# Backward of an attention and MLP block: dS of four units transposed in two transfers instead of one

## The chip, the core and the metric

The kernel runs on one core of one Trainium2 chip. A core has a matrix engine (TensorE, PE in the profile), a vector engine (VectorE, DVE), an engine for activation functions (ScalarE, ACT), a general one (GpSimd, POOL) and one that mostly issues transfers (SyncE, SP). Sixteen DMA engines move data between the chip's memory and the core's own memories, and within those; a transfer can transpose blocks of two-byte numbers on its way. The metric is the device time of one execution in microseconds. Before the change it is 2510.57 us, the median of three runs (2510.35 to 2513.57).

## The reference

One block of a transformer with adaptive layer norm is computed forward and backward, in bf16: 2048 tokens, width 512, 32 heads of 16, an MLP of width 1792. The outputs are the block's result and nine gradients. Cut to the part that matters, the forward of the attention is

```python
qkv = (x @ wqkv).reshape(B, S, 3, H, Dh)       # S = 2048, H = 32, Dh = 16
scores = jnp.einsum('bhqd,bhkd->bhqk', q, k) * scale
p = jax.nn.softmax(scores, axis=-1)
o = jnp.einsum('bhqk,bhkd->bhqd', p, v)
```

and the gradients come from `jax.vjp` of the whole block. For one head the backward needs, with P the softmax and dO the gradient of o:

- dP = dO V^T, and dS = P * (dP - the row sum of dO * O);
- dV = P^T dO and dK = dS^T Q, which contract over the queries;
- dQ = dS K, which contracts over the keys.

The matrix engine contracts over the partition dimension. dS is made with queries on the partitions, which serves dK; for dQ each 128x128 block of it has to be transposed, so that keys are on the partitions.

## The kernel before

The program runs through a forward phase, the MLP's backward, the attention's backward (`phase5` and `attn_bwd`), and a last phase with the weight gradients (`phase6`). Only the attention's backward is touched.

**Loops.** `attn_bwd` walks over 8 groups of four heads (`g`), two pairs of heads in each (`jp`), 4 chunks of 512 keys (`c`), and 16 tiles of 128 queries (`ib`). One step of the innermost loop is a *unit*: 128 queries, 512 keys, two heads (`a` = 0, 1). Four units in a row are a *group* (G = 4); there are 256 groups. Two groups in a row are a *pair*, 128 in all.

**A unit.** For each of its two heads PE makes the scores (L1601) and ACT their exponential `pu` (L1604). One unit later PE makes dP (L1522, in `dP`), and DVE multiplies it with `pu` into `ds` (L1526). In every second group (`off`) the product of unit 1, head 1, is made by ACT and POOL instead: ACT copies dP out of PSUM (L1534), POOL multiplies (L1535, in `dP_pool`). Matmuls for dK and dV follow (L1459, in `kv`).

**A group's dS.** The tile `ds` has 128 partitions (queries) and 4 units x 2 heads x 512 keys, that is 32 blocks of 128x128, eight to a unit. There are three such buffers. `dS` is called one unit behind the scores; when it is called for the last unit of a group, which is in the first unit of the next group, it issues one transposing transfer on SP (L1543) from `ds` to a tile `dsT`. In groups that are not `off` the transfer leaves out blocks 0 to 3 (unit 0, head 0): `turn_ds`, called in the third unit of a group, has PE transpose these four (L1559) and ACT copy them to `dsT` (L1560). So the transfer has 28 blocks in even groups and 32 in odd ones (`off`, where `turn_ds` only chooses the buffer). A block is 32 KB.

**dQ.** When both groups of a pair have been sent off, eight entries join the list `pendq`. `dq` takes one entry and issues four matmuls (L1484), each of which reads one half of one of the pair's two `dsT` tiles. Two entries are taken in the first and the third unit of each group, as long as more than eight are in the list. A pair's matmuls therefore begin two groups after its second transfer was issued and are spread over two groups. The last of them gives its two `dsT` tiles back to the list `dT_free`, which holds five tiles in all (four of its own, and one in the tile `keep`); `turn_ds` takes the first free one.

**The order.** PE, SP and POOL run their instructions in the order in which the program is written (a manual schedule). In this stage SP's queue holds nothing but the transfers of dS. POOL's queue holds its products and the loads for the next heads (L1590), each behind a one-element copy `tick` (L1589) that ties it to a `ds`. After the loops POOL issues eight loads of 128 KB (L1623), PE works off what is left of dK, dV and dQ between the first matmuls of the weight gradients (L1652), and DVE brings the last dQ out of PSUM (L1492).

**Waits.** The tile framework puts them in: a transfer waits for the engines that wrote its blocks and for the readers of the tile it overwrites, and a reader of `dsT` waits for the transfer that wrote the part it reads.

Of the kernel before, what the change touches and what calls it, by code (L numbers as in the profile page):

```python
# [19 lines left out]
P = 128  # L20
# [15 lines left out]
class Background:  # L36
# [13 lines left out]
    def next(self):  # L50
        while self.gens:
            r = next(self.gens[0], None)
            if r is not None:
                if isinstance(r, tuple):
                    self.mark = r[0]
                    self.seen.add(r[0])
                return r
            self.gens.pop(0)
        return None
# [46 lines left out]
class K:  # L106
# [1324 lines left out]
    def attn_bwd(self):  # L1431
# [7 lines left out]
        tc, nc = self.tc, self.nc  # L1439
        S, D, H, NQ, ST, SC = self.S, self.D, self.H, self.NQ, self.ST, self.SC  # L1440
        G = 4
# [95 lines left out]
        def dS(u):  # L1537

            (T, g, jp, c, ib, kvT, pu, dsg, i, grp) = u
            pend.append((T, g, jp, c, ib, kvT, pu, dsg[:, i]))  # L1540
            if i == G - 1:
                dsT, n = grp
                nc.sync.dma_start_transpose(dsT.rearrange("p (b k) -> p b k", k=P)[:, n:, :],  # L1543
                                            dsg[:].rearrange("p i a k -> p (i a k)")[:, n * P:])
                two.append(dsT)
                if len(two) == 2:
                    pendq.extend((T, g, jp, c, ib - 2 * G + 1, a, sub, two[:]) for a in range(2) for sub in range(4))
                    two.clear()

        def turn_ds(dsg, grp, skip, late):  # L1550

            dsT = next(t for t in dT_free if not late or t is not own)
            dT_free[:] = [t for t in dT_free if t is not dsT]
            grp.extend((dsT, 0 if skip else 4))
            if skip:
                return
            tp = stp.tile([P, 4, P], BF16, name="st")
            for b in range(4):
                nc.tensor.transpose(tp[:, b, :], dsg[:, 0, 0, b * P:(b + 1) * P], self.ident[:])  # L1559
            nc.scalar.copy(dsT[:, 0:4 * P], tp[:].rearrange("p b k -> p (b k)"))  # L1560
# [4 lines left out]
        for g in range(NQ):  # L1565
            for jp in range(2):
# [16 lines left out]
                for c in range(SC):  # L1583
                    c0 = 512 * c
                    for ib0 in range(0, ST, G):
# [5 lines left out]
                        dsg, grp = self.dsp.tile([P, G, 2, 512], BF16, name="ds"), []  # L1591
                        for i in range(G):
                            ib = ib0 + i
                            q = slice(ib * P, (ib + 1) * P)
                            if turnq and i == 3 and m >= (7 if turnq[0][2] is None else 2):
                                turn(*turnq.pop(0))
                            pu = self.pup.tile([P, 2, 512], BF16, name="pu")
                            for a in range(2):
                                stt = stp.tile([P, 512], F32, name="st")
                                rs = slice(64 * jp, 64 * jp + 64)  # L1600
                                nc.tensor.matmul(stt[:], lhsT=T["QT"][rs, q], rhs=masked["KT"][a][rs, c0:c0 + 512],  # L1601
                                                 start=True, stop=True)
                                held = dP(last, a) if last else None
                                nc.scalar.activation(pu[:, a, :], stt[:], ACT.Exp, scale=self.scale)  # L1604
                                if held is not None:
                                    dP_pool(last, held)
                                if a == 0 and i % 2 == 1 and off(c, ib) and len(pend) >= 4:
                                    kv_two(1)
                            if last:
                                dS(last)  # L1610
                            last = (T, g, jp, c, ib, kvT, pu, dsg, i, grp)
                            if i % 2 == 1 and len(pend) >= 4:
                                kv_two(1 if off(c, ib) else 2)
                            elif i % 2 == 0 and len(pendq) > 2 * G:
                                for _ in range(4 if end else 2):
                                    dq(pendq.pop(0))
                            if i == 2:
                                turn_ds(dsg, grp, off(c, ib), end and m > 2)
            T = Tn
        with tc.manual_schedule(engines=ALL):  # L1620
            for t in (2, 0):
                for p in self.wq_pieces(t):
                    nc.gpsimd.dma_start(*p)  # L1623
            for a in range(2):
                dP(last, a)
            dS(last)
            while len(pend) > 2:
                kv_two()
            kv_two(1)
            for _ in range(2 * G):  # L1630
                dq(pendq.pop(0))
            kv_two(1)
            k0, v0, k1 = [dpp.tile([P, 512], F32, name="dp") for _ in range(3)]
            self.dw_mm(k0, 1, 0, 0, ST // 2)
            turn(*turnq.pop(0))
            self.dw_mm(v0, 2, 0, 0, ST // 2)
            self.dw_mm(k0, 1, 0, ST // 2, ST)
            self.col_sum(1)
            self.dw_mm(v0, 2, 0, ST // 2, ST)
            self.col_sum(2)  # L1640
            self.cs_bc(1)
            while pendq:
                dq(pendq.pop(0))
            self.cs_bc(2)
            turn(*turnq.pop(0))
            self.dw_mm(k1, 1, 1, 0, ST)
# [312 lines left out]
```

## Time and profile before

| | |
|---|---|
| median of three runs | 2510.57 us (2510.35 to 2513.57) |
| the profiled execution | 2511.14 us, its span 2509.0 us |
| busy share of the span | PE 97%, ACT 91%, DVE 68%, POOL 29% |
| the attention's backward | first transfer of dS at 1174.8 us, last at 2385.4 us |
| transfers of dS | 256: 208 to the tiles `dsT`, 48 to the one in `keep` |
| from issue to landing, those to `dsT` | 5.0 / 6.7 / 8.8 us (least, median, greatest) |
| SP's queue held by one, the same | 3.4 / 4.1 / 6.3 us |
| data moved by DMA | 445.78 MB, of which 336.29 MB on SP's queue |

All times inside an execution are counted from the start of the span. The profile lists instructions by source line, and the same line can stand for thousands of them. "PE accq L1484 <- DMA dsT<-ds" reads: PE stood still before a matmul of line 1484 that writes `accq`, and what ended the wait was the landing of a transfer from `ds` to `dsT`. A duration of a transfer on SP's queue is the time in which the queue is held by the issue; the landing is later. The DMA share is the mean over the sixteen engines of the time that their packets took, and can exceed 1 because packets overlap; GB/s is what they moved.

### The profile page before, as it was taken

Reading aid. Unit: us, or ns where it says so; the run is one execution under the profiler, and the core shown is the slowest. Engines: PE = TensorE matmul, PEld = TensorE weight load, DVE = VectorE, ACT = ScalarE, POOL = GpSimd, SP = SyncE. Lnnn points to the kernel's source line nnn. Section 1 sums busy time; section 2 is a strip of 40 time slices with the busy share of each in tenths; the row PEclk is TensorE's granted clock in tenths of the full one; section 3 lists DMA queues with packets and bytes.
Section 4 is the critical chain, followed back from the end, with each engine's and each line's share of the span. In section 5 each row is a group of like instructions: output and inputs, shape, how many; then the busy total and the mean of one; then the engine's idle time right before and its main releaser. Section 6 shows DMA issues by size and latency. Waiting matters only on the chain.

```text
span 2509.0 us, 68721 instructions
## 1 busy us (share of the span) xinstructions
PE 2438.6 (97%) x26695; PEld 1080.0 (43%) x26695; DVE 1709.6 (68%) x3519; ACT 2295.0 (91%) x3789; POOL 716.4 (29%) x1289
## 2 busy tenths in 40 slices
PE   8999999999999999999999999999999999999998
PEld 4555555555555554573333333333333333333343
DVE  6222322422332344677999999999999999999957
ACT  7999999999999997534999999999999999999935
POOL 2344531220131022245222222222222222222223
PEclk9999999999999999999999999999999999999999
DMA  4688661441243044598999999999999999999997
GB/s 166 133 180 208 170 121 50 129 100 39 99 115 90 23 131 138 122 199 214 236 215 227 224 221 228 223 222 221 229 222 222 230 223 222 225 226 232 233 191 208
DMA packets 1260526, 445.78 MB, mean 178 GB/s; under 512 B 1204052, under 2 KB 1228246, under 8 KB 1260198
## 3 DMA queue, kind: packets, MB, share of 16 engines
q1 hardware_dynamic: 1219654, 336.29, 70.7%
q0 software_dynamic: 38464, 104.04, 13.6%
q8 instruction: 209, 3.42, 0.6%
q10 hardware_dynamic: 2080, 1.05, 0.1%
q14 instruction: 119, 0.97, 0.1%
HBM read 75.83 MB, written 64.49 MB: 56 GB/s over the span
## 4 chain that ended last, share of the span: by engine, by line
PE 58%; ACT 27%; DMA 7%; issue 4%; DVE 3%; POOL 1%; SPq 0%; DVEq 0%; ACTq 0%; POOLq 0%
ACT pu L391 18%; PE st L1601 17%; PE acckv L1459 8%; PE st L388 8%; ACT pu L1604 7%; PE accq L1484 5%; DMA dsT<-ds 3%; PE accbank L322 3%; PE dps L1050 2%; PE pps L1237 2%; PE st L1559 1%; PE dp L1522 1%; PE dp L1652 1%; DVE ds L1526 1%; DMA keep<-ds 1%
## 5 line engine op out<-in xcount | busy, mean ns | idle before, releaser
L1526 DVE TENSOR_TENSOR ds<-dp,pu 128x512 bf16<-128x512 f32 x1920 | 1181.7, 684 | 25.1 <-PE dp L1522 19.1
L1604 ACT ACTIVATE pu<-st 128x512 bf16<-128x512 f32 x2048 | 1072.7, 661 | 30.1 <-PE st L1601 21.3
L391 ACT ACTIVATE pu<-st 128x1024 bf16<-128x1024 f32 x992 | 912.2, 1077 | 5.1 <-PE st L388 4.9
L388 PE MATMUL st<-QTm,KTq 128*128 128x512 bf16 x1984 | 588.4, 377 | 20.0 <-ACT pu L391 6.0
L322 PEld LDWEIGHTS <-pu 128*128 128x128 bf16 x8192 | 347.3, 96 | 236.3 <-issue 3.2
L1522 PE MATMUL dp<-kvm,q 64*128 64x512 bf16 x1024 | 364.1, 384 | 1.5 <-DVE ds L1526 0.7
L1522 PE MATMUL dp<-kvm,dOTg 64*128 64x512 bf16 x1024 | 361.8, 384 | 0.5 <-DVE ds L1526 0.4
L322 PE MATMUL accbank<-Vaug,pu 128*128 128x17 bf16 x8192 | 357.7, 171 | 1.2 <-ACT Vaug L522 0.9
L1601 PE MATMUL st<-kvm,q 64*128 64x512 bf16 x1024 | 351.6, 381 | 6.0 <-ACT pu L1604 0.2
L1601 PE MATMUL st<-kvm,QTg 64*128 64x512 bf16 x1024 | 350.6, 381 | 6.8
L388 PEld LDWEIGHTS <-KTq 128*128 128x128 bf16 x1984 | 188.2, 96 | 177.5 <-issue 125.6
L1535 POOL TENSOR_TENSOR ds<-junk,pu 128x512 bf16<-128x512 f32 x64 | 73.8, 1153 | 372.2 <-ACT junk L1534 302.4
L1459 PE MATMUL acckv<-ds,Qg 128*16 128x512 bf16 x1024 | 176.0, 382 | 0.2
L1459 PE MATMUL acckv<-pu,dOg 128*16 128x512 bf16 x1024 | 175.9, 382 | 0.0
L1459 PE MATMUL acckv<-ds,q 128*16 128x512 bf16 x1024 | 175.8, 382 | 0.0
L1459 PE MATMUL acckv<-pu,q 128*16 128x512 bf16 x1024 | 175.8, 382 | 0.0
L1535 POOL TENSOR_TENSOR ds<-csq,pu 128x512 bf16<-128x512 f32 x64 | 73.8, 1154 | 349.6 <-ACT csq L1534 271.5
L302 POOL DMA_DIRECT2D QTm<-QTq_d x124 | 63.8, 516 | 341.5 <-PE st L388 319.9
L1601 PEld LDWEIGHTS <-q 64*128 64x128 bf16 x1024 | 66.9, 94 | 159.6 <-issue 144.0
L1601 PEld LDWEIGHTS <-QTg 64*128 64x128 bf16 x1024 | 67.0, 94 | 158.2 <-issue 141.3
L329 DVE RECIPROCAL rl<-accbank 128x4 f32<-128x4 f32 x128 | 23.0, 179 | 159.0 <-PE accbank L322 158.8
L1522 PEld LDWEIGHTS <-q 64*128 64x128 bf16 x1024 | 89.8, 93 | 56.7 <-issue 50.4
(390 smaller groups left out, 3197.0 us busy)
## 6 DMA issues: line engine op xcount, KB each, us to landing
KTq<-KTq_d POOLq DMA_DIRECT2D x24, 512.0 KB, 3.8
duT_d<-auT POOLq DMA_DIRECT2D x3, 1792.0 KB, 7.6
aT_d<-rT POOLq DMA_DIRECT2D x3, 1792.0 KB, 11.0
KTq_d<-KTq SPq DMA_DIRECT2D x32, 128.0 KB, 2.1
QTq_d<-ev_fm SPq DMA_DIRECT2D x32, 128.0 KB, 4.3
ktm_d<-ev_tm POOLq DMA_DIRECT2D x32, 128.0 KB, 2.5
VTq_d<-vT POOLq DMA_DIRECT2D x4, 1024.0 KB, 6.2
dx<-dx_d SPq DMA_DIRECT2D x16, 256.0 KB, 5.3
```

The source lines that it names most:

```text
L302: nc.gpsimd.dma_start(QTm[j][32 * j:32 * j + 32, :], self.QTq_d[g, 32 * j:32 * j + 32, 512 * qc:512 * (qc + 1)])
L322: nc.tensor.matmul(acc[:, a, sub, :], lhsT=pu[:, a, sub * P:(sub + 1) * P], rhs=Vaug[:, kb, h, :], start=(kb == 0 and a == 0 and sub == 0) ...
L388: nc.tensor.matmul(stt[:, a, :], lhsT=KT[:, kb * P:(kb + 1) * P], rhs=QTm[2 * jp + a][:], start=True, stop=True)
L391: nc.scalar.activation(pu[:], stt[:], ACT.Exp, scale=self.scale)
L1050: nc.tensor.matmul(pt[:], lhsT=a[st], rhs=g_tm[:, st, :], start=(st == 0), stop=(st == ST - 1))
L1459: nc.tensor.matmul(acckv[r:r + DH, :], lhsT=T[n][:, ib, col:col + DH], rhs=src[:, a, :], start=(ib == 0), stop=(ib == ST - 1))
L1484: nc.tensor.matmul(accq[r:r + 32, o:o + 256], lhsT=T["K"][:, 4 * c + sub, col:col + 32], rhs=v[:, r // 32 % 2 * 2:r // 32 % 2 * 2 + 2, 4 * ...
L1522: nc.tensor.matmul(dp[:], lhsT=T["dOT"][rd, ib * P:(ib + 1) * P], rhs=masked["VT"][a][rd, 512 * c:512 * (c + 1)], start=True, stop=True)
L1526: nc.vector.tensor_tensor(dsg[:, i, a], dp[:], pu[:, a, :], ALU.mult)
L1535: nc.gpsimd.tensor_tensor(dsg[:, i, 1], f[:], pu[:, 1, :], ALU.mult)
L1601: nc.tensor.matmul(stt[:], lhsT=T["QT"][rs, q], rhs=masked["KT"][a][rs, c0:c0 + 512], start=True, stop=True)
L1604: nc.scalar.activation(pu[:, a, :], stt[:], ACT.Exp, scale=self.scale)
```

## The change

The one transfer of a group becomes two. The first carries units 0 and 1 (12 blocks where the first four go over PE, else 16) and is issued in `turn_ds`, in the third unit of the group, ahead of PE's four transposes. The second carries units 2 and 3 (16 blocks) and is issued where the one transfer was. A helper `cross` issues both. The matmuls of dQ, the buffers and the order on the other engines stay as they are.

```diff
             if i == G - 1:
                 dsT, n = grp
-                nc.sync.dma_start_transpose(dsT.rearrange("p (b k) -> p b k", k=P)[:, n:, :],
-                                            dsg[:].rearrange("p i a k -> p (i a k)")[:, n * P:])
+                cross(dsg, dsT, 4 * G, 8 * G)
                 two.append(dsT)
...
+        def cross(dsg, dsT, a, b):
+            nc.sync.dma_start_transpose(dsT.rearrange("p (b k) -> p b k", k=P)[:, a:b, :],
+                                        dsg[:].rearrange("p i a k -> p (i a k)")[:, a * P:b * P])
+
         def turn_ds(dsg, grp, skip, late):
 
             dsT = next(t for t in dT_free if not late or t is not own)
             dT_free[:] = [t for t in dT_free if t is not dsT]
             grp.extend((dsT, 0 if skip else 4))
+            cross(dsg, dsT, grp[1], 4 * G)
             if skip:
                 return
```

## The prediction

> **What bounds the kernel now.** I read the profile in this order: busy time by stage, then the waits inside the stage that the change touches, then the transfer itself (how long it takes, what the DMA engines move meanwhile), then the tail of the stage. The stage is the attention backward, from about 1175 to 2390 us.
>
> Busy time by engine in a stretch of it (columns: stretch, length, busy us of each engine with instruction counts, granted clock, DMA share, GB/s):
>
> ```profile
> 1180.00:2384.00 1204.00, 1185.66 (x12962) 385.25 (x12958) 1179.06 (x1917) 1194.81 (x2438) 313.61 (x627) 1.00 1.18 225
> ```
>
> ScalarE (fourth) is busy for 1194.81 of 1204 us; TensorE, 1185.66, and VectorE, 1179.06, are close behind. No engine can lose work through this change, so what it can give is waits. The waits of ACT and PE on others in the same stretch, and the longest of SP's queue (total us, times, longest):
>
> ```profile
> ACT pu L1604 <- PE dp L1522: 5.3, 12, 0.9
> PE accq L1484 <- DMA dsT<-ds: 3.8, 8, 0.9
> PE accq L1484 <- DMA keep<-ds: 0.9, 2, 0.5
> SPq L1543 <- DVE ds L1526: 584.9, 226, 5.4
> ```
>
> ACT stands still for 5.3 us in the whole stage. PE has ten waits on a landing dS, together 4.7 us, and they stand behind ACT's: the matmuls of dQ (L1484) hold up the scores that ACT needs. SP has time: its queue waits 584.9 us for VectorE. Then the transfer: the transposes of dS, 28 or 32 blocks of 128x128, beside a small transpose of 4 blocks from the forward (columns of the first two kinds of line: duration min/median/max in ns, here the time that SP's queue is held; the last is issue to landing in us):
>
> ```profile
> L1543 SPq DMA_TRANSPOSE dsT<-ds x208: 3399/4099/6260, 1174.8 to 2385.4; - x104
> DMA to landing us min/median/max: 5.0/6.7/8.8
> L646 SPq DMA_TRANSPOSE ev_tm<-KTq x32: 1189/1202/2556, 61.2 to 244.2; - x32
> DMA to landing us min/median/max: 2.3/3.2/5.4
> ```
>
> The shortest landings give (5.0 - 2.3) / (28 - 4) = 0.11 us a block, and 2.3 - 4 x 0.11 = 1.85 us that does not depend on size. One such transfer, with a product of POOL that its group needs, in half-microsecond stretches:
>
> ```profile
> 1603.88 1.15 POOL L1535 TENSOR_TENSOR ds<-csq,pu 128x512 bf16<-128x512 f32 x1 [5.44 <-ACT csq L1534]
> ...
> 1605.97 4.81 SPq L1543 DMA_TRANSPOSE dsT<-ds  x1
> ```
>
> ```profile
> 1606.00:1606.50 0.50, 0.50 (x11) 0.20 (x4) 0.50 (x2) 0.50 (x2) 0.00 (x0) 1.00 0.34 81
> 1606.50:1607.00 0.50, 0.50 (x12) 0.12 (x8) 0.50 (x2) 0.50 (x2) 0.18 (x1) 1.00 0.30 107
> ...
> 1608.50:1609.00 0.50, 0.50 (x8) 0.20 (x4) 0.50 (x2) 0.50 (x2) 0.00 (x0) 1.00 0.03 3
> 1609.00:1609.50 0.50, 0.50 (x12) 0.12 (x8) 0.50 (x2) 0.50 (x2) 0.00 (x0) 1.00 0.09 10
> ...
> 1610.00:1610.50 0.50, 0.48 (x6) 0.18 (x3) 0.50 (x2) 0.50 (x2) 0.00 (x0) 1.00 1.28 291
> ...
> 1612.50:1613.00 0.50, 0.50 (x10) 0.16 (x6) 0.50 (x1) 0.50 (x3) 0.00 (x0) 1.00 1.33 247
> ```
>
> Read the last column. After the issue at 1605.97 the rate is low for a microsecond, there is a second hole at 1608.5 to 1609.5, and then 290 GB/s. The next transfer, issued at 1610.88 while this one was still moving, leaves hardly a hole where it takes over (247 at 1612.5). Holes belong to a start from rest. Last, the end of the stage, in the chain that ended last and in PE's timeline: the final dQ matmuls wait for the final transfer.
>
> ```profile
> 2385.37 14.00 DMA dsT<-ds
> ```
>
> ```profile
> 2399.41 1.05 PE L1484 MATMUL accq<-dsT,Kg 128*32 128x256 bf16 x30 [2.52 <-DMA dsT<-ds]
> ```
>
> **The change part by part.** A group of four units lasts 1210.6 us / 255 = 4.75 us (first to last issue of L1543), a pair of groups 9.5. The instructions of PE, ACT, DVE and POOL and their order do not change; SP gets 256 transposes more.
>
> *The earlier first half.* In even groups it has 12 blocks and is ready when DVE has made units 0 and 1, two units or 2.4 us ahead of the end. In odd groups it has 16 blocks and needs POOL's half of unit 1: in the rows above that ends at 1603.88 + 1.15 = 1605.03, only 0.94 us before the issue at 1605.97. The odd group is the one that counts: its dS is wanted two groups (9.5 us) after its last matmul, the even group's one group later still.
>
> *The landing of the pair's last blocks.* The 32 blocks of the odd group start 0.94 us earlier and follow each other at 0.11 us a block, so the end moves forward by 0.94 less what the second start costs. That is 0.1 us if it is queued behind the first (rate 247 instead of 290 for half a microsecond: 0.07), and 0.6 if it leaves half of the one-microsecond hole. Ends: a gain of 1.8 us (16 blocks x 0.11, the whole first half out of the way) and a loss (below, the second rival). I take 0.7, near the queued row, since the second half will be issued while the first still moves.
>
> *The waits in the stage.* With 0.7 us less, all waits of PE on dS up to 0.7 go and one of 0.9 leaves 0.2; of ACT's 5.3 us I take 4.4 as gained. Bounds: 0 and 5.3. What is late next is ACT itself.
>
> *The tail.* PE waits 2.52 us for a transfer that takes 14.00 us beside eight loads of 128 KB (POOL, L1623), with which it shares the engines whatever the order. I take 0.6, nearly the 0.7 above; bounds 0 and 2.5.
>
> *SP.* Two issues of at least 1.19 us (the 4-block row) in place of one of 3.4 to 4.1. If the hold goes with the blocks still to be moved, the sum stays near 4.1 of 4.75 us; nothing but these transposes is in SP's queue in this stage, so the second half waits behind the first and nobody else does. In odd groups the first half also waits for the dQ matmuls that have just freed its buffer; they precede POOL's product by over a microsecond.
>
> *Waits on other engines.* The first ds of a buffer on DVE, POOL's product and the dQ matmuls wait for two transfers instead of one. A satisfied wait is a semaphore instruction of some 20 ns that runs under the one before it (DVE is busy 98% with a wait at every instruction), so nothing. PE's transposes of unit 0 and ACT's copy to blocks 0 to 3 write other blocks than the first half; nothing.
>
> *Sum.* 4.4 + 0.6 = 5.0 us. The profiled execution took 2511.14 us (span 2509.0), 0.57 over the median of 2510.57. Against it 2506.1; against the median 2505.6. A measurement of this kernel can tell about 0.2%, 5.0 us, from no change, so this lies on the edge of it.
>
> *A rule against the change.* The Trainium skill, "DMA: Bandwidth & Descriptors" (Rules for kernel authors), says to coalesce many small transfers into one, and under "Anatomy of one DMA" gives about 2.0 us fixed for a transfer, for a software-generated one. That agrees with the 1.85 us from the rows. By the page alone 256 transfers more would be 512 us of fixed cost, if none of it overlapped; by the rows, where SP is free at 3.4 us and the blocks land at 5.0, most of it lies beside the transfer before.
>
> **The rivals.**
>
> *The DMA engines become the bound (slower).* A pair moves 60 blocks, 60 x 0.11 = 6.75 us; all traffic is 225 GB/s x 9.5 us = 2.14 MB, of which the blocks are 1.97, so loads take 0.17 MB or 0.6 us at 290 GB/s. That leaves 9.5 - 6.75 - 0.6 = 2.15 us, now filled with the holes of two transfers. With four transfers the point is 2.15 / 4 = 0.54 us a transfer: under it all is as above, over it each pair is late and PE, ACT and DVE wait for dS every time. At 0.6 us a start the price is 4 x 0.6 - 2.15 = 0.25 us a pair, over 128 pairs 32 us: 2542. At 1.07 (what two starts cost now) it would be 273 us. For it: the stage already moves 225 of 290 GB/s, and loads of POOL come in at the joints. Against it: the joint at 1612.5.
>
> *It is hidden anyway, or does not do what it says.* In odd groups the head start is only 0.94 us; if the joint eats it (0.6 for a hole, 0.3 for a load that slips between the halves), the landing does not move and neither do the waits. Time 2510 +- 3.
>
> *All waits go.* 5.3 + 2.5 = 7.8 us, 2502.8: the first half clears the way entirely. The 14.00 us at the tail, shared with loads, speaks against the second part.
>
> **How the numbers follow.** Waits go, mostly or all: 0.52, times 2502.5 to 2508, of which 0.32 is beyond 0.2%. Hidden: 0.18, nearly all within 0.2%. DMA bound: 0.30, from 2512 up, 0.28 of it beyond. Together faster 0.32, same 0.39, slower 0.29. The range begins at all waits gone, 2502.8, rounded down; upwards I leave out about half of the DMA case, that beyond 0.58 us a start (4 x 0.58 - 2.15 = 0.17, x 128 = 22 us): 2533. The likeliest case by itself is 2502.5 to 2508.
>
> **What would show it.** Right: twice the issues on the transpose's line, landings of the second half at 4 to 6 us, the ten waits of PE on dS down to one or two, ACT's 5.3 us under 1.5, the tail's 2.52 us under 2. Wrong: PE's wait on dS in tens of microseconds with landings of 8 us and more and a GB/s that stays near 225 (the DMA bound), or the same ten waits (hidden). The price of a joint between two halves is the step most likely to fail.

## The result, and the profile after

The changed kernel takes 2515.64 us (median of 20 runs, 2509.49 to 2521.17) where the kernel before took 2509.80 (20 runs beside them, 2502.70 to 2516.53). The ratio is 1.0021, 95% interval 1.0013 to 1.0030: some 5.3 us slower (5.8 by the medians). The prediction was 2505.6, 5.0 us faster; its range (2502.5 to 2533) holds the time, its direction is wrong.

The profiled execution after is the shortest of its twenty (2509.49 us, span 2507.7), 1.65 us under that of before. So the two are compared by stage, not by span, and the trace shows less of the loss than the median has. From the start to the first exponential of the backward (L1604, now L1608): 1168.31 before, 1165.62 after; nothing was changed there. From the first to the last of these exponentials: 1215.17 and 1218.40, that is 3.2 us longer. From there to the end: 125.54 and 123.71.

After, the stretch of the prediction's first view (columns as there):

```profile
1180.00:2384.00 1204.00, 1183.14 (x12938) 384.11 (x12935) 1174.72 (x1913) 1192.05 (x2431) 311.51 (x625) 1.00 1.20 225
```

ACT, the fourth, is busy for 2.8 us less of the same 1204. After, the waits of the same stretch (total us, times, longest):

```profile
ACT pu L1608 <- PE dp L1522: 7.8, 13, 1.8
PE accq L1484 <- DMA dsT<-ds: 5.6, 9, 1.4
SPq L1550 <- DVE ds L1526: 703.6, 372, 4.1
SPq L1550 <- POOL tick L1593: 171.1, 117, 3.6
```

PE's waits on dS have not gone: nine as against ten, 5.6 us as against 4.7, and the longest is 1.4 instead of 0.9. ACT's went from 5.3 to 7.8. After, the transfers of dS to `dsT` and to `keep`, and, from PE's timeline, the wait of the last dQ matmuls:

```profile
L1550 SPq DMA_TRANSPOSE dsT<-ds x416: 1404/2097/6597, 1169.8 to 2390.2; - x139
L1550 SPq DMA_TRANSPOSE keep<-ds x96: 1397/2398/4167, 1190.9 to 2309.8; - x96
...
DMA to landing us min/median/max: 3.4/4.2/6.3
```

```profile
2398.78 1.03 PE L1484 MATMUL accq<-dsT,Kg 128*32 128x256 bf16 x29 [1.17 <-DMA dsT<-ds]
```

Twice the issues, each half as long and landing sooner, and the tail's wait is 1.17 us instead of 2.52. So the change does what it says. The time by head group (from its first exponential to the next one's first, worked out from the trace's records of that line, us) shows that it gains and loses:

| head group | 1 | 2 to 6 together | 7 | 8 | sum |
|---|---|---|---|---|---|
| before | 150.46 | 757.96 | 151.31 | 155.45 | 1215.17 |
| after | 151.30 | 756.00 | 153.10 | 157.99 | 1218.40 |
| after less before | +0.8 | -2.0 | +1.8 | +2.5 | +3.2 |

In the five middle head groups the prediction's mechanism is there, at 0.4 us a head group. It is lost in the first and the last two. ACT's waits for dP over the same stretches go the same way: 2.4 to 0.8 us in the middle five; 0.4 to 1.4, none to 0.9 and 2.4 to 4.7 in the first, seventh and eighth. In the eighth the loads are mostly two to three times as large as elsewhere (256 to 384 KB a pair of groups against 128 to 144, by the packets of POOL's queue in the trace); in the first, two pairs of sixteen have 512. The seventh's are like those of the middle, and size does not explain its loss. A stretch of the eighth head group (it begins at 2228.0 before and at 2226.0 after), before and then after, with ACT's busy time fourth:

```profile
2265.00:2365.00 100.00, 96.26 (x1052) 32.60 (x1048) 95.08 (x154) 97.59 (x199) 25.79 (x51) 1.00 1.24 234
```

```profile
2265.00:2365.00 100.00, 95.25 (x1020) 31.87 (x1016) 92.27 (x150) 94.65 (x192) 23.47 (x49) 0.98 1.19 226
```

**What runs full.** SP's queue, in its timeline: the transfers of the last eight pairs, the row with the time from the first issue to the end of the last (start, length, number). Before, then after:

```profile
2312.83 78.55 SPq L1543 DMA_TRANSPOSE dsT<-ds  x16
```

```profile
2312.70 84.07 SPq L1550 DMA_TRANSPOSE dsT<-ds  x32
```

The same blocks take 5.5 us longer. Of the 78.55 us the queue is held for 69.19 (the sum of the sixteen durations); of the 84.07, for 80.68, and between one transfer and the next in the same queue there are never less than 0.04 us and mostly 0.09, which makes another 2.9 with 32. Next to nothing is left, while the engines moved no more than before (226 GB/s against 234 in the eighth head group's rows above). Over the whole stage, by the same sums: holds of 8.34 us a pair before and 1.17 free; after 8.96 and 0.62, of which 4 x 0.09 = 0.36 cannot be used. The prediction had read 584.9 us of waiting on SP as time to spare. That was a misreading which the rows themselves could have shown: with the tick's row, here of before,

```profile
SPq L1543 <- POOL tick L1589: 119.3, 124, 2.2
```

the waits add up to 704 us, and the holds in the same 1204 us to some 1056. Together that is more than there is. The view counts a wait up to the last update of the semaphore before the transfer's end, and DVE goes on updating it: the transfer that holds the queue from 1601.54 to 1605.19 was let go by the update at 1601.52, and the view takes the one at 1604.68. By the trace 570 of the 704 us lie inside the hold of the very transfer that is listed as waiting. The holds themselves contain no such wait: wherever the queue had stood still before a transfer, it went on within 0.06 us of an update that the transfer waits for. The time to spare was about 148 us, 1204 less 1056.

From this came the theory that the runs tested (called S in the expectations; A is an earlier form of it): transposes pass one at a time through SP's queue, which was 88% held; each joint adds to the holds, and where loads add more, the queue falls behind. Its rivals: B, the second half is stuck behind a first half that waits for POOL; C, a price per transfer that lies evenly over the stage and does not depend on loads.

### The profile page after: what moved, and what is told of

It is laid out like the page before. It is cut to its first block, busy times and chain, and to the rows that moved or that the text cites. A ratio compares the mean times of both kernels' runs of the same rounds, so it can differ in the third digit from the quotient of the medians.

```text
span 2507.7 us, 69254 instructions
## 1 busy us (share of the span) xinstructions
PE 2419.2 (96%) x26467; PEld 1077.5 (43%) x26695; DVE 1710.8 (68%) x3519; ACT 2295.2 (92%) x3789; POOL 713.5 (28%) x1289
## 4 chain that ended last, share of the span: by engine, by line
PE 52%; ACT 34%; DMA 7%; issue 5%; DVE 2%; POOL 1%; SPq 0%; ACTq 0%; DVEq 0%; POOLq 0%
ACT pu L391 25%; PE st L1605 18%; PE acckv L1459 8%; ACT pu L1608 6%; PE accq L1484 5%; PE st L388 4%; DMA dsT<-ds 3%; PE accbank L322 2%; PE dps L1050 2%; PE st L1563 2%; PE dp L1522 1%; PE dps L995 1%; PE dp L1656 1%; PE st L1751 1%; PE pps L1237 1%
## 5 line engine op out<-in xcount | busy, mean ns | idle before, releaser
L1608 ACT ACTIVATE pu<-st 128x512 bf16<-128x512 f32 x2048 | 1074.3, 666 | 32.4 <-PE st L1605 21.3
L388 PE MATMUL st<-QTm,KTq 128*128 128x512 bf16 x1859 | 560.7, 377 | 27.0 <-ACT pu L391 6.1
```

The costliest lines, as they stand in the source:

```text
L388: nc.tensor.matmul(stt[:, a, :], lhsT=KT[:, kb * P:(kb + 1) * P], rhs=QTm[2 * jp + a][:], start=True, stop=True)
```

## The experiments

Ratios are to the kernel before on the same chip, with their 95% intervals; its medians there were 2508.72, 2508.88, 2508.79, 2509.24 and 2510.55 us.

**Four transfers a group.**

```diff
             if i == G - 1:
...
-                cross(dsg, dsT, 4 * G, 8 * G)
+                cross(dsg, dsT, 6 * G, 8 * G)
...
-            cross(dsg, dsT, grp[1], 4 * G)
+            cross(dsg, dsT, grp[1], 2 * G)
+            cross(dsg, dsT, 2 * G, 4 * G)
```

(and one of blocks 16 to 23 in the fourth unit)

> Four transfers per group, one for each unit: the first two issued one after the other in the third unit, the third in the fourth unit, the last at the end; twice the joints of the change. Theory A: joints of a pair rise from 4 to 8; by the trace of after, where a pair's drains lie 0.2 us apart and PE's slack at its median is 1.05 us, the DMA engines run out of reserve: PE waits on dS in every pair, 30 to 150 us slower. Theory B: the first two transfers of odd groups still wait for POOL's product, the last two follow: like the change, 3 to 8 us slower. Theory C: 3 x 5.3 = 16 us slower.

Measured: 2773.72 us, ratio 1.1051 (1.1033 to 1.1069), 265 us slower. Its transfers to `dsT`, and a stretch of SP's timeline:

```profile
L1552 SPq DMA_TRANSPOSE dsT<-ds x832: 1195/1260/3419, 1170.9 to 2663.5; - x167
```

```profile
2303.72 23.74 SPq L1552 DMA_TRANSPOSE dsT<-ds  x16
```

A transfer of 8 blocks holds the queue for 1.26 us, hardly more than one of 4 (1.20 at least). Sixteen follow each other in 23.74 us: the queue never waits. Over the stage the holds are 10.86 us a pair, and with the 0.81 between them 11.67 against the 9.42 that ACT needs (150.7 us for 16 pairs in the quietest head groups); 128 x 2.25 = 288 us, near the 265 measured. That SP's queue is a server that can run full, and what happens then, is shown. It is not the engines' rate that ends here: from 1180 to 2384 us they move 183 GB/s, where before the change they moved 225. The granted clock fell too, to 0.93 in this stretch, but PE is busy for only 1053 of its 1204 us. The expectation of 30 to 150 us was too low, since it had no floor of 1.2 us in it. B, which expected 3 to 8 us, falls.

**Only the even groups, only the odd ones.**

```diff
+            if not skip:          # e_odd: if skip
+                cross(dsg, dsT, grp[1], 4 * G)
...
-                cross(dsg, dsT, 4 * G, 8 * G)
+                cross(dsg, dsT, 4 * G if n else 0, 8 * G)     # e_odd: 4 if n else 4 * G
```

> Two transfers only in even groups (12 + 16 blocks), one of 32 blocks in odd ones. The change cost 5.3 us. Theory A (every joint between transposes lets waiting loads in and costs a hole; the reserve of a pair is lost where loads are large): half of the joints added, so about half of the loss: 2 to 3 us slower than before, PE's wait on dS in the stage 4.5 to 5.5 us. Theory B (in odd groups the second half is stuck on SP behind a first half that waits for POOL's product): no loss here, 0 us, or up to 3 us faster, since even groups get their head start for nothing. Theory C (a fixed price per transfer wherever it is): half of the loss, 2.6 us, spread evenly over the stage.

> Two transfers only in odd groups (16 + 16 blocks), one of 28 blocks in even ones. Theory A: 2 to 3 us slower than before, as with the split in even groups alone. Theory B: the whole loss of 5.3 us or more, with SP held 4 us and more by the second half. Theory C: 2.6 us slower, evenly over the stage.

Measured: even alone 2514.77 us, ratio 1.0020 (1.0010 to 1.0030), the whole loss; odd alone 2506.49, ratio 0.9991 (0.9979 to 1.0002), if anything faster. B had it the other way round. A and C, which gave each half of the loss, are wrong too. What separates them is the landing. From the landing of a pair's last transfer to PE's first dQ matmul of that pair there are, at the median, 0.64 us before, 0.72 with the even split, 1.38 with the odd one, 1.07 with both (this matmul reads the even group's tile, so it can come before the landing; the figures serve for comparison). Only the odd group's transfer is waited for, so only its split can gain. The even one adds to the holds alone: 8.61 us a pair instead of 8.34. That these holds are what it costs is argued and not shown: the odd split adds more to them (8.71 us a pair) and is not slower. In the execution profiled, the odd split took 4.1 us off the five middle head groups and put 9.4 on the other three; its median shows that other executions lose less there. How often such stalls come was not settled.

**The loads left out.**

```diff
+                if 1 <= g < NQ - 1:
+                    pieces, later = [], []
```

> The kernel before without the loads of the next heads in the second to seventh group of heads (six of eight), so the later heads work on data that is left over; the transfers of dS and all other work stay. It is the base for the same change with the split. Theory A: loads broke in at the joints, so PE's waits on dS shrink outside the first and the last group of heads, 2 to 4 us faster than before. Theory C: no difference in the waits of dS, 0 to 1 us.

> The changed kernel with the same loads left out. To be compared with the kernel before without these loads. Theory A: without loads that break in at the joints the split costs nothing in these six groups of heads: the two kernels differ by less than 1.5 us there, and what is left of the loss lies in the eighth group of heads, where loads are still there (2 to 4 us). Theory C: the split still costs 5 us. Theory B: the split still costs about 5 us, all over the stage.

In a second pair the loads of the eighth head group are replaced as well:

```diff
-                            nc.gpsimd.dma_start(*pieces.pop(0))
+                            if g == NQ - 1:
+                                nc.gpsimd.memset(pieces.pop(0)[0], 0.0)
+                            else:
+                                nc.gpsimd.dma_start(*pieces.pop(0))
```

> The kernel before without loads after the first group of heads: those of the second to seventh are left out, those of the eighth (wq, WmT, xhat) are replaced by setting their tiles to zero on POOL, so outputs that depend on them are not computed. Theory S: SP's free time per pair rises from 1.17 to 1.5 us in the last group of heads too, PE's waits on dS there go: 3 to 5 us faster than before.

> The changed kernel with the same loads left out or replaced; to be compared with the kernel before without them. Theory S and theory L: without loads the reserve is 1.0 us a pair with the split and 1.3 without it, enough for both; the landing comes 0.7 us earlier, waits on dS under 1 us outside the first group of heads: the split is level with or 1 to 3 us faster than the one transfer. If the joints cost time by themselves: the split is still 5 us slower.

Measured, one transfer and two: 2507.43, ratio 0.9993 (0.9981 to 1.0005), and 2509.58, 0.9998 (0.9987 to 1.0009), with the eighth's loads kept; 2506.07, 0.9989 (0.9980 to 0.9999), and 2504.93, 0.9982 (0.9971 to 0.9994), without them. So the split's loss, 5.8 us by the medians, is 2.2 where the second to seventh head group have no loads and turns to a gain of 1.1 where the eighth has none either, both within what the intervals leave open; the traces are clearer. Without the loads (the second pair) head groups 2 to 6 take 754.99 us with one transfer and 754.18 with two; the eighth 153.43 and 152.46, where with loads it was 155.45 and 157.99. The seventh, which lost 1.8 us with loads, gains 0.4 without them (151.27 to 150.85, in both pairs of kernels), so its loss goes with loads too. The first, whose loads are there in all four, still loses with the split: 151.69 and 154.33. The last eight pairs on SP's queue without loads, one transfer and then two:

```profile
2308.77 79.01 SPq L1543 DMA_TRANSPOSE dsT<-ds  x16
```

```profile
2310.41 80.05 SPq L1550 DMA_TRANSPOSE dsT<-ds  x32
```

Of these the queue is held for 65.17 and 64.36 us. Sixteen loads of 128 KB add 69.19 - 65.17 = 4.0 us of holds with one transfer a group, and 80.68 - 64.36 = 16.3 with two: 0.25 and 1.0 us a load. Over the stage the loads add 0.40 us a pair (7.94 to 8.34) and 0.98 (7.98 to 8.96). C falls: in the second pair the two joints of a pair cost SP's queue 0.04 us of holds on the mean of the stage and the 0.18 between. Even the 0.04 belongs to the first head group, which has its loads (8.14 to 9.18); in the other seven the holds fall from 7.91 to 7.81.

**The same cuts, both halves written at the group's end.**

```diff
-                cross(dsg, dsT, 4 * G, 8 * G)
+                cross(dsg, dsT, n, 4 * G)
+                cross(dsg, dsT, 4 * G, 8 * G)
...
-            cross(dsg, dsT, grp[1], 4 * G)
```

> Two transfers per group as in the change, but both issued at the group's end: the joints without the head start. Theory S (transposes pass one at a time through SP's queue: its holds and the 0.09 us between two add up to 8.5 us of a pair's 9.5 before, to 9.3 after; the joints eat the reserve): holds of a pair near 8.9 us as after, and since no half starts early, PE's slack on the landing falls from 0.64 us (median of before) to 0.3 or less: PE's waits on dS 10 to 30 us, 8 to 25 us slower than before. Theory H (joints are free, the harm comes from the early half of even groups, which goes ahead of loads that would have slipped in there): level with before, within 2 us. Theory L (only loads of the last group of heads make the loss): 5 us slower, as the change.

Measured: 2518.62 us, ratio 1.0032 (1.0018 to 1.0046). The time is as S said, but not for its reason: holds of 8.92 us a pair and a landing 1.13 us ahead of PE, much as after (8.96 and 1.07). This was no test. On SP nothing stands between the two places, and a transfer waits for the engines that wrote its own blocks, not for its place in the program; the first half goes out as early as before. It serves as a second look at the changed program: head groups 1, 2 to 6, 7 and 8 take 152.18, 755.93, 152.24 and 157.74 us. The pattern of after is there in a second execution too.

**Another cut: 24 and 8 blocks, in odd groups alone.**

```diff
+            if i == G - 2 and not grp[1]:
+                cross(dsg, grp[0], 0, 6 * G)
...
-                cross(dsg, dsT, 4 * G, 8 * G)
+                cross(dsg, dsT, n or 6 * G, 8 * G)
...
-            cross(dsg, dsT, grp[1], 4 * G)
```

> Two transfers only in odd groups, cut later: 24 blocks (three units) in the fourth unit, the last 8 at the end; even groups one of 28. Theory S: one joint per pair as with 16 + 16, but the last transfer is half as long (8 blocks hold SP for 1.26 us where 16 took 2.56), so the pair lands some 0.5 to 1 us earlier than with 16 + 16 (slack median 1.38 us there): slack 1.8 us or more, PE's waits on dS under 3 us, 2 to 5 us faster than before. If the head start is worth nothing and the joint costs (theory L or a price per joint alone): 1 to 3 us slower than before.

Measured: 2504.63 us, ratio 0.9980 (0.9970 to 0.9991), 4.2 us faster than before. Its waits in the stage, and its last eight pairs on SP's queue:

```profile
ACT pu L1609 <- PE dp L1522: 2.5, 8, 0.5
PE accq L1484 <- DMA dsT<-ds: 1.9, 5, 0.6
```

```profile
2307.46 77.33 SPq L1552 DMA_TRANSPOSE dsT<-ds  x24
```

The holds there are 69.88 us, as with one transfer a group (69.19). The eighth head group takes 152.92 us instead of 155.45. The landing is 1.34 us ahead, not the 1.8 expected, so the gain in the middle (756.88 against 757.96) is smaller than with 16 and 16.

**dQ taken later.** The other way to give the landing more time is to take the entries of `pendq` later:

```diff
-                                for _ in range(4 if end else 2):
+                                for _ in range(4 if end else (0, 2, 3, 3)[m % 2 * 2 + i // 2]):
```

with one transfer, with two, and with one and K, Q and dO loaded in pieces of 512 columns:

> One transfer per group as before, but the entries of dQ are taken later: over the four places of a pair 0, 2, 3 and 3 instead of 2 each, so that the first dQ matmul of a pair comes one place, 2.4 us, later. If PE's waits on dS, and ACT's behind them, are lateness of the landing alone (theory A, where both the before and the change run short of reserve): PE's 4.7 us of waits on dS and ACT's 5.3 us in the stage go to under 1 us, and the kernel is 3 to 5 us faster than before. If they are put down to the wrong cause (dQ's own place in PE's order, dT buffers that come free later): 0 us, or slower by 2 to 10 us because the buffers are given back later and SP waits for them.

> The changed kernel (two transfers) with the entries of dQ taken later (0, 2, 3, 3). Theory A: 2.4 us more reserve covers the worst late landing of after (1.87 us), so PE's waits on dS go and the kernel is level with the one that takes dQ later with one transfer, 3 to 5 us faster than before. If the joints make the DMA engines the bound throughout (the rival of the prediction): lateness adds up and is not covered, still 3 us or more slower than before.

> One transfer per group, dQ's entries taken later, and the loads of K, Q and dO in pieces of 512 columns (128 KB) instead of 256 (64 KB), half as many. Theory A: fewer loads break in at joints, but each is longer; with 2.4 us of reserve neither shows: within 1 us of the kernel that only takes dQ later. If every load that breaks in costs a hole that matters: 1 to 3 us faster than it.

Measured: 2513.96 us, ratio 1.0020 (1.0008 to 1.0031); 2525.77, 1.0065 (1.0053 to 1.0077); 2518.81, 1.0039 (1.0024 to 1.0055). What theory A expected missed in all three. The times of the first two lie in the other branch that each expectation names (2 to 10 us slower; 3 us or more slower), but the first not for the reason given there: no wait of SP's queue on the dQ matmuls is listed. The waits of ACT with one transfer:

```profile
ACT dsT L1560 <- PE st L1559: 2.3, 2, 2.2
ACT pu L1604 <- PE dp L1522: 0.3, 1, 0.3
ACT kvT L1462 <- PE acckv L1459: 0.3, 1, 0.3
```

PE's waits on dS are gone and ACT's fell from 5.3 to 2.9 us, yet the stage is 2.9 us longer (1218.11). Each middle head group takes 0.3 us more. The work of PE is the same in another order, with 12 dQ matmuls together where there were 8; that this spacing is the reason was not tested. With two transfers the waits of the eighth head group, from 2265 us on, show where a late queue comes back:

```profile
PE dp L1522 <- DVE ds L1526: 8.1, 5, 5.8
DVE ds L1526 <- DMA dsT<-ds: 7.6, 2, 6.0
ACT dsT L1564 <- PE st L1563: 6.6, 1, 6.6
```

DVE waits 6.0 us to overwrite a `ds` that its transfer has not read yet; PE and then ACT stand behind it. The holds there are 10.27 us a pair. Taking dQ later hides a late landing but not a full queue.

**Why a load costs more with the split.** Loads moved from the first to the third unit of a group, on the changed kernel and on the cut of 24 and 8; and the loads of xhat halved (the loop that spreads them sends 31 of the 32 halves, so the last is left out):

```diff
+                            while i == 2 and pieces and (total - len(pieces)) * SC * ST <= m * G * total:
...
-                        while pieces and (total - len(pieces)) * SC * ST <= m * G * total:
```

```diff
-                    pieces = [(self.xhat1_6[:, st, :], ...[:, st, :])
-                              for st in range(ST)]
+                    pieces = [(self.xhat1_6[r:r + 64, st, :], ...[r:r + 64, st, :])
+                              for st in range(ST) for r in (0, 64)]
```

> The changed kernel with the loads of the next heads issued in the third unit of a group instead of the first. By the runs so far, a 128 KB load costs SP's queue some 1 us of hold in the last eight pairs with four transfers a pair (80.7 us of holds with loads, 64.4 without, 16 loads) and 0.25 us with two. If that is because the load, issued with the group's last half, comes in exactly between the two halves of an odd group (theory J): the holds of the last eight pairs fall from 80.7 to 75 us or less and the kernel is 2 to 5 us faster than the changed one. If it is only that SP's queue has no free time left for the load's bytes and its start wherever it comes (theory F): holds stay at 79 to 82 us, 4 to 10 us slower than before, as the change.

> 24 + 8 blocks in odd groups, one transfer in even ones, and the loads in the third unit. Theory J: nothing to gain, since the 24 blocks are sent before the load comes in either way; or worse, since a load now stands in front of them: 0 to 3 us slower than 24 + 8 alone (2504.6). Theory F: the same as 24 + 8 alone within 1.5 us.

> The changed kernel with the 16 loads of 128 KB in the second half of the last group of heads (xhat) cut in two by partitions, 32 of 64 KB. Theory F: the bytes are the same and the breaks twice as many; if the break costs (a hole per load): holds of the last eight pairs rise from 80.7 to 85 us or more, 2 to 5 us slower than the change. If the length of one load is what delays the next half: holds fall to 75 us or less, 2 to 5 us faster than the change.

Measured: 2523.47 us, ratio 1.0052 (1.0039 to 1.0064); 2520.02, 1.0040 (1.0027 to 1.0054); 2518.66, 1.0038 (1.0024 to 1.0052). Moving the loads is much worse with either cut, by more than any expectation had, and why was not found. In the changed kernel the holds of the last eight pairs fall to 77.5 us, between the two expectations (75 and 79), while those of the middle head groups rise from 8.77 to 9.06 a pair. Halves hold 77.7 us: neither the number of breaks nor the length of one explains the price by itself. That a load costs more with the split is shown; how it lengthens a hold stays open.

**Each cut where it gains.**

```diff
-                cross(dsg, dsT, 4 * G, 8 * G)
+                cut = n or (6 * G if g in (0, NQ - 2, NQ - 1) else 4 * G)
+                if not n:
+                    cross(dsg, dsT, 0, cut)
+                cross(dsg, dsT, cut, 8 * G)
...
-            cross(dsg, dsT, grp[1], 4 * G)
```

> Odd groups in two transfers, even ones in one, and the cut chosen by the head group: 24 + 8 blocks in the first, seventh and eighth, where loads are large or the stage begins, 16 + 16 in the five between. By the profiled executions, 16 + 16 in odd groups alone took 4.1 us off the five middle head groups and put 9.4 us on the other three; 24 + 8 took 1.1 us off the middle ones and 3.0 off the others. If the two add: 7 us off the stage and 1 to 3 more at its tail: 5 to 9 us faster than before, 1 to 4 us faster than 24 + 8 everywhere. If the large stalls of 16 + 16 in the first and last head groups were chance of one execution (its median was 2.2 us faster than before): no better than 24 + 8 everywhere, 3 to 5 us faster than before.

Measured: 2501.46 us (12 runs), ratio 0.9965 (0.9951 to 0.9978): 9 us faster than before, the fastest of all. Its stage is 4.7 us shorter (1210.43), not 7: the middle head groups take 755.55 us, 2.4 less, the other three 2.3 less. After the last exponential this execution is another 3.4 us shorter (125.54 to 122.12). Its waits in the stage:

```profile
ACT pu L1610 <- PE dp L1522: 2.8, 4, 1.2
PE accq L1484 <- DMA dsT<-ds: 2.6, 3, 1.3
```

## Why the prediction was wrong

**The step that failed** is the one on SP: "If the hold goes with the blocks still to be moved, the sum stays near 4.1 of 4.75 us", with "SP has time" before it. The hold does not go with the blocks alone. A group's sum came to 4.48 us on the mean (half of 8.96; 4.17 before), and with the 0.09 after each transfer to 4.66 of the 4.79 that a group then lasted. By the means over the stage an even group's holds go from 3.92 to 1.60 + 2.40 = 4.00 us, an odd one's from 4.42 to 2.51 + 2.46 = 4.96, and each extra transfer adds 0.09: 0.17 and 0.63 us, 0.8 a pair, out of 1.0 that could be used (1.17 less 2 x 0.09). In the eighth head group the holds rise from 8.70 to 9.83 us a pair, past the 9.4 of ACT.

**The price of a joint**, 0.1 us, read from one place at 1612.5, is the same error in the landing's step: 0.17 and 0.63. The prediction had named it as the step most likely to fail, but looked for it in a start from rest. There was no rest: before the change, 92% of the odd groups' transfers and 99% of the even ones' were issued before the last packets of the transfer ahead (by the packets in the trace, in order).

**The earlier first half**: an even group's was to start 2.4 us ahead. It mostly starts when the queue comes free: nine times in ten within 0.10 us of the end of the transfer ahead.

**The landing**, 0.7 us, was 0.43 at the median (0.64 to 1.07): right in kind. Without loads after the first head group it is 0.6 (1.9 to 2.5, one transfer and two), near the 0.7. In the eighth head group it is a loss, 0.56 to 0.19.

**The waits in the stage**, 4.4 of ACT's 5.3 us, is the term that fell: they rose to 7.8. The gain is there in the middle, 2.0 us, and 5.2 are lost in the other three head groups (0.8, 1.8 and 2.5). **The tail**, 0.6 us, was 1.35 (2.52 to 1.17).

**The rivals.** "The DMA engines become the bound" had the right shape, and its point, 0.54 us a transfer, is about what the joints cost in the eighth head group: (9.83 - 8.70) / 2 = 0.57. It was wrong to be thought of as all over the stage or nowhere; it holds where loads are large, so it costs 5 us and not 32. What is full is seen at SP's queue; whether engines behind it set the holds was not separated. That the range holds the time is owed to this rival alone, for which its upper part was left. And by the signs set down beforehand the change would have passed for "hidden", with nine waits of PE where there were ten: but the landing did move, and the waits moved from the middle of the stage to its ends.

The rule that spoke against the change, to coalesce many small transfers (the Trainium skill, "DMA: Bandwidth & Descriptors", Rules for kernel authors), was right in direction for this change, though 24 and 8 blocks, with 128 transfers more than before, were faster. The 2.0 us of fixed cost that the page gives for a software-generated transfer ("Anatomy of one DMA") is not what a transfer more costs here: 256 more took 1147.1 - 1067.1 = 80 us of SP's queue, 0.31 each, and 0.09 between.

## What to carry to other kernels

Before a transfer is cut in two, add up how long its queue is held in the stage; a wait that the profile lists for a queue is no time to spare, since here four fifths of it lay inside the holds of the waiting transfers themselves. Cut only the transfer that somebody waits for; where loads are large, the short last piece (24 and 8) did better here than halves, and in the middle of the stage halves did. Look at the stretch with the largest loads first: with the change the queue was held for 93% of the stage on the mean (1147 of 1227 us) and was full there.

## What the runs showed of the hardware

- The hold of a transpose on SP's queue has a floor: the shortest seen are 1.19 us for 4 blocks, 1.23 for 8, 1.39 for 12 and 1.59 for 16; 2.93 for 24, 3.36 for 28 and 3.84 for 32.
- The first packets come 1.17 us after the issue or later, in every kernel here.
- Loads of another queue lengthen these holds, and by more where the same blocks are cut into two transfers a group: 0.25 us a load of 128 KB with one, 1.0 with two (the last eight pairs).
- SP's queue can run full while the sixteen engines move less than they can: with four transfers a group they moved 183 GB/s in the stage, with one 225.
